# Order of the first loads, one decay on ScalarE and a two-bank last output in a retention + gated MLP kernel

## The chip, the cores and the metric

The kernel runs on 1 core of a Trainium2 chip. The metric is the device time of one execution in microseconds, and a kernel's time is the median over several executions. The engines named below are PE (TensorE, matrix multiply; PEld is its weight load), DVE (VectorE), ACT (ScalarE), POOL (GpSimd) and SP (SyncE, which here only issues DMAs). DMAs issued by SP and ACT go through the hardware queues, those issued by POOL through the software queue.

## The reference

A retention recurrence over q, k, v of shape (batch 4, heads 8, sequence 768, head dimension 64), followed by a two-layer network on the 3072 tokens:

```python
gamma = 1.0 - 2.0 ** (-5.0 - np.arange(H))
scale = 1.0 / np.sqrt(D)
for t in range(S):
    state = gamma[None, :, None, None] * state + np.einsum('bhd,bhe->bhde', k[:, :, t], v[:, :, t])
    y[:, :, t] = scale * np.einsum('bhd,bhde->bhe', q[:, :, t], state)
x = y.transpose(0, 2, 1, 3).reshape(B * S, H * D)     # 3072 x 512
h = x @ w_in                                          # 512 x 2048
g = h * np.cos(h)
out = g @ w_out                                       # 2048 x 512
```

Inputs and output are float32; the matrix work is done in bf16.

## The kernel before

The recurrence is computed in chunks of C = 128 positions. A *pair* p is one chunk of two batches (b = 0 and 1); there are 12 pairs, and six per couple of batches. Two pairs make a *group* g of 512 tokens for the network; there are 6 groups. The order of all instructions on each engine is the order in which the code issues them: nothing reorders them, and each engine works its own list in order.

For one pair:

- `load` (L108, its DMA at L113) brings q, k or v of one batch, 128 positions x 8 heads x 64, 256 KB.
- `conv_q` (L163) multiplies q by gamma^t times the scale, `conv_v` (L168) multiplies v by gamma^-t, `conv_k` (L174) casts k to bf16. gq and gk are small tables of [128 positions, chunk, head]. In the start, q is done by DVE, k by ACT and v by POOL.
- `stage_t` (L189) transposes q and k on PE, four transposes for q and four for k of each batch; `copy_bits` (L179) brings them from PSUM to SBUF on DVE. `stage_a` (L215) multiplies keys by queries, `stage_m` (L223) puts the causal mask on the product on DVE, four operations per pair.
- `half_y` (L236, L241) computes one batch's output of the pair on PE from the masked product, the decayed v and, from the second chunk on, the state; ACT copies it as `xt` (L245). `stage_s` (L257) adds to the state, which is copied at L262.

For the network: `unit_f` (L284) is one 128-row block of the hidden layer for a whole group, `pair_f` (L296) the same for one pair's 256 tokens, two blocks at a time; `act` takes the cosine on ACT (L275) and the product on DVE (L279). `unit_o` (L310) is a quarter of one 128-token block of the output; after the fourth quarter ACT copies it (L322) and SP sends it (L323). The very last block is copied in two halves of 256 columns, one by DVE (L317) and sent by SP (L318), one by ACT (L319) and sent by ACT (L320); both halves lie in one PSUM bank.

The weights come from POOL's queue, cast to bf16 on the way: `load_w_in(r)` (L118) brings a quarter of w_in, `load_w_out(r)` (L123) a quarter of w_out. `warm(n)` (L332) is n matmuls of 512 columns on zeros into a spare bank, which fill waits of PE.

The start, in the order of the code: SP loads pair 0's q0, k0, q1 and pair 1's q0; POOL loads pair 0's k1, computes two small position tables (iota), then loads pair 0's v0, v1 and pair 1's q1, k0, k1, v0, v1, then the first slice of w_in, then multiplies pair 0's v0 and v1, loads two more slices of w_in, multiplies pair 1's v0 and v1, and goes on with the last slice, w_out and pair 2. On PE: eight fillers, pair 0's transposes with fillers between, its products, its outputs, pair 1's transposes and products, then pair_f(0, 0) and half_y(1, b) in turns, stage_s(1), pair_f(1, 0), and from there unit_f and unit_o without a stop. After 48 us the transposes of later pairs are DMA transposes on SP.

PSUM banks are handed out by a first-in first-out list (`Banks`). A DMA of POOL's queue uses one of eight semaphores in turn, so that its ninth DMA waits for the first to have landed.

Of the kernel before, what the change touches and what calls it, by code (L numbers as in the profile page):

```python
# [12 lines left out]
AF = mybir.ActivationFunctionType  # L13
# [17 lines left out]
def kernel(  # L31
# [9 lines left out]
    nc = tc.nc  # L41
    B, H, S, D = q.shape
    C = 128
    NC = S // C
# [4 lines left out]
    KOUT = DF // 128  # L49
    NP = B // 2 * NC  # L50
    NG = NP // 2
# [3 lines left out]
    scale = 1.0 / math.sqrt(D)  # L55
# [8 lines left out]
    def sb(shape, dt, name):  # L64
        return const.tile(shape, dt, name=name)

    banks = Banks([psum.tile([128, 512], FP32, name=f"bank{i}") for i in range(7)])
# [10 lines left out]
    w_out_sb = sb([128, KOUT, DM], BF16, "w_out_sb")  # L78
# [4 lines left out]
    vf = [[sb([128, H, D], FP32, f"vf{i}_{b}") for b in range(2)] for i in range(PRE)]  # L83
    ob = [sb([128, DM], FP32, f"ob{i}") for i in range(4)]
    NB = 3
    qk = [sb([128, 2, 2, H, D], BF16, f"qk{i}") for i in range(NB)]
    vs = [sb([128, 2, H, D], BF16, f"vs{i}") for i in range(NB)]
# [5 lines left out]
    gt = [sb([128, KOUT, 4 * C], BF16, f"gt{i}") for i in range(2)]  # L93
# [5 lines left out]
    gk = sb([128, NC, H], FP32, "gk")  # L99
# [8 lines left out]
    def load(eng, p, names):  # L108
        bp, c = divmod(p, NC)
        for n in names:  # L110
            t, src = SRC[n[0]]
            b = int(n[1])
            eng.dma_start(  # L113
                out=t[SLOT[p]][b],
                in_=src[2 * bp + b, :, ds(c * C, C)].rearrange("h t d -> t h d"))

    def load_w_in(r):
        nc.gpsimd.dma_start(  # L118
            out=w_in_sb[r],
            in_=moe_w_in[:, ts(r, 512)].rearrange("(i p) f -> p i f", p=128))  # L120
# [6 lines left out]
    def w_in_t(i, f):  # L127
        return w_in_sb[f // 4][:, i].rearrange("p (m j) -> p j m", j=4)[:, f % 4, :]


    load(nc.sync, 0, ("q0", "k0", "q1"))
    load(nc.sync, 1, ("q0",))
    load(nc.gpsimd, 0, ("k1",))
    nc.gpsimd.iota(pos, pattern=[[C, NC]], base=1, channel_multiplier=1,
                   allow_small_or_imprecise_dtypes=True)
    nc.gpsimd.iota(rel, pattern=[[1, 128]], base=0, channel_multiplier=-1,
                   allow_small_or_imprecise_dtypes=True)
    load(nc.gpsimd, 0, ("v0", "v1"))
    load(nc.gpsimd, 1, ("q1", "k0", "k1"))
    nc.vector.memset(zero, 0.0)  # L140
    nc.vector.memset(lnsc, math.log(scale))
    nc.vector.memset(halfpi, math.pi / 2.0)
# [15 lines left out]
    def bc(g, c):  # L158
        return g[:, c, :].unsqueeze(2).to_broadcast([128, H, D])
# [6 lines left out]
    def conv_v(p, eng, bs=(0, 1), g=None):  # L166
        for b in bs:
            eng.tensor_tensor(out=vs[p % NB][:, b], in0=vf[SLOT[p]][b],  # L168
                              in1=bc(gk if g is None else g, p % NC), op=ALU.mult)
# [8 lines left out]
    def copy_bits(out, bank):  # L178
        nc.vector.tensor_scalar(out=out.bitcast(mybir.dt.uint32),  # L179
                                in0=bank.bitcast(mybir.dt.uint32),  # L180
                                scalar1=0, scalar2=None, op0=ALU.bitwise_or)

    def stage_t(p, b, fill=0):
        n = p % NB
        bank = banks.take()
        tr = bank.bitcast(BF16).rearrange("p (w a t) -> p w a t", w=2, a=HP)
        for w in range(2):
            for a in range(HP):
                nc.tensor.transpose(tr[:, w, a, :], qk[n][:, b, w, 2 * a : 2 * a + 2, :], ident)  # L189
            if w == 0:  # L190
                warm(fill)
        copy_bits(qkt[n][:, b], tr)
        banks.give(bank)
# [8 lines left out]
    def qt(n, b, a):  # L202
        return qkt[n][:, b, 0, a, :]
# [16 lines left out]
    def stage_m(p, item, parts=(0, 1)):  # L220
        b, bk, ap = item
        for j in parts:
            nc.vector.tensor_tensor(  # L223
                out=am[p % 2][b][j], in0=ap[j],
                in1=mask.unsqueeze(1).to_broadcast([128, HP, 128]), op=ALU.mult)
            banks.give(bk[j])

    def half_y(p, b):
        c = p % NC
        n = p % NB  # L230
        bank = banks.take()
        yp = bank.rearrange("p (a t) -> p a t", a=HP)
        for a in range(HP):
            if c > 0:
                for j in range(2):
                    nc.tensor.matmul(  # L236
                        yp[ts(j, 64), a, :], lhsT=stb[p % 2][:, b, a, ts(j, 64)],
                        rhs=qt(n, b, a), start=True, stop=False,
                        skip_group_check=True)
            for j in range(2):  # L240
                nc.tensor.matmul(  # L241
                    yp[ts(j, 64), a, :], lhsT=vs[n][:, b, 2 * a + j, :],
                    rhs=am[p % 2][b][j][:, a, :], start=(c == 0), stop=True,
                    skip_group_check=True)
        nc.scalar.copy(out=xt[(p // 2) % 2][:, :, ts(2 * (p % 2) + b, C)], in_=yp)  # L245
        banks.give(bank)
# [25 lines left out]
    def act(bank, out):  # L272
        cb = cosb[f_no[0] % 3]
        f_no[0] += 1
        nc.scalar.activation(out=cb, in_=bank, func=AF.Sin, bias=halfpi)  # L275
        if len(out.shape) == 3:
            cb = cb.rearrange("p (f t) -> p f t", f=2)
            bank = bank.rearrange("p (f t) -> p f t", f=2)
        nc.vector.tensor_tensor(out=out, in0=bank, in1=cb, op=ALU.mult)  # L279
# [9 lines left out]
    def pair_f(p, r, parts=(0, 1)):  # L289

        g, hf = divmod(p, 2)
        for f in [4 * r + 2 * i for i in parts]:
            bank = banks.take()
            for e in range(2):
                for i in range(KIN):
                    nc.tensor.matmul(bank[:, ts(e, 256)], lhsT=w_in_t(i, f + e),  # L296
                                     rhs=xt[g % 2][:, i, ts(hf, 256)],
                                     start=(i == 0 and e == 0), stop=(i == KIN - 1),
                                     skip_group_check=True)
            act(bank, gt[g % 2][:, f : f + 2, ts(hf, 256)])  # L300
            banks.give(bank)
# [3 lines left out]
    def unit_o(g, j, part):  # L305
        if part == 0:
            o_bank[j] = banks.take()
        bank = o_bank[j]
        for f in range(4 * part, 4 * part + 4):
            nc.tensor.matmul(bank, lhsT=gt[g % 2][:, f, ts(j, 128)], rhs=w_out_sb[:, f, :],  # L310
                             start=(f == 0), stop=(f == KOUT - 1))
        if part == 3:
            o = ob[j % 4]
            bp, c = divmod(2 * g + j // 2, NC)
            dst = out[ds((2 * bp + j % 2) * S + c * C, C), :]
            if g == NG - 1 and j == 3:
                nc.vector.tensor_copy(out=o[:, ts(0, 256)], in_=bank[:, ts(0, 256)])  # L317
                nc.sync.dma_start(out=dst[:, ts(0, 256)], in_=o[:, ts(0, 256)])  # L318
                nc.scalar.copy(out=o[:, ts(1, 256)], in_=bank[:, ts(1, 256)])  # L319
                nc.scalar.dma_start(out=dst[:, ts(1, 256)], in_=o[:, ts(1, 256)])  # L320
            else:
                nc.scalar.copy(out=o, in_=bank)  # L322
                nc.sync.dma_start(out=dst, in_=o)  # L323
            banks.give(bank)

# [2 lines left out]
    def warm(n):  # L330
        for _ in range(n):
            nc.tensor.matmul(spare, lhsT=zero[:, :128], rhs=zero, start=True, stop=True,  # L332
                             skip_group_check=True)

    def attend(p):
        for it in [stage_a(p, b) for b in range(2)]:
            stage_m(p, it)

    load(nc.gpsimd, 1, ("v0", "v1"))
    load_w_in(0)  # L340
    conv_v(0, nc.gpsimd)
    load_w_in(1)
    load_w_in(2)

    warm(8)
    conv_q(0, nc.vector)
    conv_k(0, True)
    stage_t(0, 0, 3)
    warm(2)
    stage_t(0, 1)  # L350
    a00 = stage_a(0, 0)
    stage_m(0, a00)
# [25 lines left out]
    warm(1)  # L378
    banks.give(spare)
    pair_f(0, 0, (0,))  # L380
    half_y(1, 0)
    pair_f(0, 0, (1,))
    half_y(1, 1)
    stage_s(1, nc.scalar.copy)
    pair_f(1, 0)
# [78 lines left out]
    for g in range(2, NG + 1):  # L464
        for s in range(16):
            hf, r = divmod(s, 8)
            p = 2 * (g + 1) + hf
            if g == 2 and s % 2 == 0:
                unit_o(1, *divmod(8 + s // 2, 4))
            if g < NG:  # L470
                unit_f(g, s)
            if g > 2:
                unit_o(g - 1, *divmod(s, 4))
            if p < NP:
                if r == 0:
                    ahead(p + 1)
                elif r == 1:
                    todo = [stage_a(p, b) for b in range(2)]
                    stage_m(p, todo[0])
                    if p + 1 < NP:  # L480
                        stage_t_dma(p + 1)
                elif r == 2:
                    stage_m(p, todo[1])
                elif r == 5:
                    later(p)
# [30 lines left out]
```

## Time and profile before

| what | value |
|---|---|
| median of 6 runs | 211.1 us (210.83 to 211.58) |
| the profiled execution | 211.16 us, of which the span is 209.4 us |
| mean granted TensorE clock | 0.996 |
| PE busy (share of the span) | 200.2 us (96%) |
| DVE, ACT, POOL busy | 114.8, 111.7, 91.9 us |
| HBM read, written | 27.26 MB, 6.29 MB |

The span runs from the first to the last instruction; the rest of the time lies around it. Times in the profile's rows are microseconds from the span's start. A busy row of PE is from a matmul's start to its modelled end, so that neighbouring matmuls overlap: 512 columns have a mean of 379 ns, while 16 of them in a row take about 3.45 us.

The first 30 us are also full of DMA: the page's 40 slices (5.2 us each) show 145, 335, 253, 207, 217 and 251 GB/s for the first six.

### The profile page before, as it was taken

The numbers are of one execution on the slowest core, as the hardware profiler recorded it, in microseconds if no ns is written. First come the engines' busy times: TensorE is split into PE (matmuls) and PEld (weight loads), VectorE is DVE, ScalarE is ACT, GpSimd is POOL, SyncE is SP. The second block draws the span as 40 slices with busy tenths as digits, with TensorE's granted clock in tenths as the row PEclk, the third lists the DMA queues.
The fourth block names the chain that finished last, engine by engine and source line by source line (L and its number), as shares of the span: only waits on it lengthen the run. The fifth ranks groups of instructions, "written<-read, shape, count | busy, mean of one in ns | idle before, by whom it ended". The sixth has DMA issues, their size and how long they took to land.

```text
span 209.4 us, 4140 instructions
## 1 busy us (share of the span) xinstructions
PE 200.2 (96%) x1613; PEld 112.3 (54%) x1637; DVE 114.8 (55%) x190; ACT 111.7 (53%) x181; POOL 91.9 (44%) x105
## 2 busy tenths in 40 slices
PE   7789999999999999999999999999999999999992
PEld 3258554558897554555545455455455444444440
DVE  5695785363967737859575475485382334443000
ACT  6266774237998336766745745735535553553110
POOL 7998238399997944999973400000000000000000
PEclk9999999999999999999999999999999999999998
DMA  6999999999999999999997171171101101110121
GB/s 145 335 253 207 217 251 288 333 247 333 237 254 214 223 308 279 210 274 237 285 185 178 58 95 52 51 102 50 50 3 50 50 13 41 50 50 29 73 89 64
DMA packets 49124, 33.83 MB, mean 162 GB/s; under 512 B 40080, under 2 KB 42384, under 8 KB 49104
## 3 DMA queue, kind: packets, MB, share of 16 engines
q1 hardware_dynamic: 42192, 15.86, 34.7%
q0 software_dynamic: 6768, 17.57, 31.0%
q8 instruction: 13, 0.21, 0.4%
q10 hardware_dynamic: 144, 0.13, 0.2%
q14 instruction: 7, 0.06, 0.1%
HBM read 27.26 MB, written 6.29 MB: 160 GB/s over the span
## 4 chain that ended last, share of the span: by engine, by line
PE 90%; POOL 3%; DMA 3%; issue 1%; ACT 0%; DVE 0%; POOLq 0%; DVEq 0%
PE bank L310 40%; PE bank L284 31%; PE bank L296 9%; DMA w_in<-in_moe_w_in_dram 3%; PE bank L236 3%; PE bank L215 3%; PE bank L241 2%; POOL vf L113 2%; POOL kf L113 1%; PE st_ps L257 1%; PE bank L189 1%; POOL qf L113 0%; ACT xt L245 0%; DVE ob L317 0%; ACT ob L319 0%
## 5 line engine op out<-in xcount | busy, mean ns | idle before, releaser
L279 DVE TENSOR_TENSOR gt<-bank,cosb 128x512 bf16<-128x512 f32 x96 | 65.7, 690 | 64.3 <-ACT cosb L275 63.9
L275 ACT ACTIVATE cosb<-bank,halfpi 128x512 bf16<-128x512 f32 x96 | 65.6, 687 | 52.4 <-PE bank L284 41.3
L310 PE MATMUL bank<-w_out_sb,gt 128*128 128x512 bf16 x372 | 91.8, 379 | 1.1 <-issue 0.5
L284 PE MATMUL bank<-xt,w_in 128*128 128x512 bf16 x294 | 73.7, 380 | 0.4
L310 PEld LDWEIGHTS <-gt 128*128 128x128 bf16 x384 | 36.7, 98 | 42.8
L284 PEld LDWEIGHTS <-w_in 128*128 128x128 bf16 x304 | 33.8, 114 | 30.8 <-issue 0.2
L223 DVE TENSOR_TENSOR am<-bank,mask 128x512 bf16<-128x512 f32 x48 | 30.3, 682 | 0.4 <-PE bank L215 0.2
L163 POOL TENSOR_TENSOR qk<-qf,gq 128x512 bf16<-128x512 f32 x18 | 19.1, 1081 | 15.1 <-DMA qf<-in_q_dram 15.0
L322 ACT COPY ob<-bank 128x512 f32<-128x512 f32 x23 | 13.4, 587 | 21.7 <-PE bank L310 21.4
L168 POOL TENSOR_TENSOR vs<-vf,gk 128x512 bf16<-128x512 f32 x22 | 22.5, 1046 | 0.1
L113 POOL DMA_DIRECT2D vf<-in_v_dram x23 | 20.3, 887 | 4.9 <-DMA w_out_sb<-in_moe_w_out_dram 4.9
L113 POOL DMA_DIRECT2D kf<-in_k_dram x23 | 20.8, 908 | 2.0 <-DMA w_out_sb<-in_moe_w_out_dram 1.2
L174 ACT CAST qk<-kf 128x512 bf16<-128x512 f32 x24 | 13.9, 614 | 11.8 <-DMA kf<-in_k_dram 11.6
L296 PE MATMUL bank<-xt,w_in 128*128 128x256 bf16 x160 | 18.7, 273 | 0.7 <-ACT xt L245 0.4
L296 PEld LDWEIGHTS <-w_in 128*128 128x128 bf16 x160 | 17.1, 114 | 1.5 <-DMA w_in<-in_moe_w_in_dram 0.6
L245 ACT CAST xt<-bank 128x512 bf16<-128x512 f32 x24 | 13.0, 587 | 3.0 <-DVE gt L279 3.0
L241 PE MATMUL bank<-am,vs 128*64 128x128 bf16 x192 | 11.7, 220 | 0.7 <-POOL vs L168 0.7
L241 PEld LDWEIGHTS <-vs 128*64 128x64 bf16 x192 | 9.9, 110 | 2.1 <-POOL vs L168 2.1
L236 PEld LDWEIGHTS <-stb 128*64 128x64 bf16 x160 | 8.6, 109 | 4.0 <-issue 3.5
L236 PE MATMUL bank<-qkt,stb 128*64 128x128 bf16 x160 | 10.5, 222 | 0.0
L262 DVE CAST stb<-st_ps 64x512 bf16<-64x512 f32 x12 | 8.2, 687 | 3.5 <-PE st_ps L257 3.3
L332 PE MATMUL bank<-gt 128*128 128x512 bf16 x19 | 7.8, 525 | 1.4 <-DVE gt L140 1.2
(36 smaller groups left out, 65.0 us busy)
## 6 DMA issues: line engine op xcount, KB each, us to landing
kf<-in_k_dram POOLq DMA_DIRECT2D x23, 256.0 KB, 5.6
vf<-in_v_dram POOLq DMA_DIRECT2D x23, 256.0 KB, 6.8
out_dram<-ob SPq DMA_DIRECT2D x23, 256.0 KB, 2.0
qf<-in_q_dram SPq DMA_DIRECT2D x19, 256.0 KB, 6.7
w_in<-in_moe_w_in_dram POOLq DMA_DIRECT2D x4, 512.0 KB, 8.1
w_out_sb<-in_moe_w_out_dram POOLq DMA_DIRECT2D x4, 512.0 KB, 12.5
qf<-in_q_dram POOLq DMA_DIRECT2D x5, 256.0 KB, 7.5
kf<-in_k_dram SPq DMA_DIRECT2D x1, 256.0 KB, 4.8
```

Source lines behind the costliest of these rows:

```text
L113: eng.dma_start(out=t[SLOT[p]][b], in_=src[2 * bp + b, :, ds(c * C, C)].rearrange("h t d -> t h d"))
L163: eng.tensor_tensor(out=qk[p % NB][:, b, 0], in0=qf[SLOT[p]][b], in1=bc(gq, p % NC), op=ALU.mult)
L168: eng.tensor_tensor(out=vs[p % NB][:, b], in0=vf[SLOT[p]][b], in1=bc(gk if g is None else g, p % NC), op=ALU.mult)
L174: nc.scalar.copy(out=qk[p % NB][:, b, 1], in_=kf[SLOT[p]][b])
L223: nc.vector.tensor_tensor(out=am[p % 2][b][j], in0=ap[j], in1=mask.unsqueeze(1).to_broadcast([128, HP, 128]), op=ALU.mult)
L236: nc.tensor.matmul(yp[ts(j, 64), a, :], lhsT=stb[p % 2][:, b, a, ts(j, 64)], rhs=qt(n, b, a), start=True, stop=False, skip_group_check=True)
L241: nc.tensor.matmul(yp[ts(j, 64), a, :], lhsT=vs[n][:, b, 2 * a + j, :], rhs=am[p % 2][b][j][:, a, :], start=(c == 0), stop=True, skip_grou ...
L275: nc.scalar.activation(out=cb, in_=bank, func=AF.Sin, bias=halfpi)
L279: nc.vector.tensor_tensor(out=out, in0=bank, in1=cb, op=ALU.mult)
L284: nc.tensor.matmul(bank, lhsT=w_in_t(i, f), rhs=xt[g % 2][:, i, :], start=(i == 0), stop=(i == KIN - 1))
L296: nc.tensor.matmul(bank[:, ts(e, 256)], lhsT=w_in_t(i, f + e), rhs=xt[g % 2][:, i, ts(hf, 256)], start=(i == 0 and e == 0), stop=(i == KIN ...
L310: nc.tensor.matmul(bank, lhsT=gt[g % 2][:, f, ts(j, 128)], rhs=w_out_sb[:, f, :], start=(f == 0), stop=(f == KOUT - 1))
```

## The change

Four things:

- The hardware queue brings only pair 0's q0 and k0 in the start. POOL's queue brings, in this order, pair 0's q1, (the two iotas,) pair 0's k1, v0, v1, pair 1's q0, k0, q1, k1, the first slice of w_in, then, behind the multiply of pair 0's v1, pair 1's v0 and v1, and the next two slices of w_in.
- Pair 0's v0 is multiplied by ACT, in eight operations of one head each, behind the casts of pair 0's k; v1 stays on POOL.
- Two fillers of PE go (one in pair 0's first stage_t, one behind it), and pair_f(0, 0) does both its halves ahead of half_y(1, 0).
- The last 128-token block of the output is no longer four quarters of unit_o into one bank: `last_o` takes 320 columns into one bank and then 192 columns into another. ACT copies and SP sends the first, DVE copies and ACT sends the second.

```diff
-    load(nc.sync, 0, ("q0", "k0", "q1"))
-    load(nc.sync, 1, ("q0",))
-    load(nc.gpsimd, 0, ("k1",))
+    load(nc.sync, 0, ("q0", "k0"))
+    load(nc.gpsimd, 0, ("q1",))
     nc.gpsimd.iota(pos, pattern=[[C, NC]], base=1, channel_multiplier=1,
                    allow_small_or_imprecise_dtypes=True)
     nc.gpsimd.iota(rel, pattern=[[1, 128]], base=0, channel_multiplier=-1,
                    allow_small_or_imprecise_dtypes=True)
-    load(nc.gpsimd, 0, ("v0", "v1"))
-    load(nc.gpsimd, 1, ("q1", "k0", "k1"))
+    load(nc.gpsimd, 0, ("k1", "v0", "v1"))
+    load(nc.gpsimd, 1, ("q0", "k0", "q1", "k1"))
+    load_w_in(0)
...
-            if g == NG - 1 and j == 3:
-                nc.vector.tensor_copy(out=o[:, ts(0, 256)], in_=bank[:, ts(0, 256)])
-                nc.sync.dma_start(out=dst[:, ts(0, 256)], in_=o[:, ts(0, 256)])
-                nc.scalar.copy(out=o[:, ts(1, 256)], in_=bank[:, ts(1, 256)])
-                nc.scalar.dma_start(out=dst[:, ts(1, 256)], in_=o[:, ts(1, 256)])
+            nc.scalar.copy(out=o, in_=bank)
+            nc.sync.dma_start(out=dst, in_=o)
+            banks.give(bank)
+
+    def last_o(g, j):
+        bp, c = divmod(2 * g + j // 2, NC)
+        dst = out[ds((2 * bp + j % 2) * S + c * C, C), :]
+        for i, (a, n) in enumerate(((0, 320), (320, 192))):
+            bank = banks.take()
+            for f in range(KOUT):
+                nc.tensor.matmul(bank[:, :n], lhsT=gt[g % 2][:, f, ts(j, 128)],
+                                 rhs=w_out_sb[:, f, ds(a, n)],
+                                 start=(f == 0), stop=(f == KOUT - 1))
+            o = ob[i]
+            if i:
+                nc.vector.tensor_copy(out=o[:, :n], in_=bank[:, :n])
+                nc.scalar.dma_start(out=dst[:, ds(a, n)], in_=o[:, :n])
             else:
-                nc.scalar.copy(out=o, in_=bank)
-                nc.sync.dma_start(out=dst, in_=o)
-            banks.give(bank)
+                nc.scalar.copy(out=o[:, :n], in_=bank[:, :n])
+                nc.sync.dma_start(out=dst[:, ds(a, n)], in_=o[:, :n])
...
+    conv_v(0, nc.gpsimd, (1,))
     load(nc.gpsimd, 1, ("v0", "v1"))
-    load_w_in(0)
-    conv_v(0, nc.gpsimd)
     load_w_in(1)
     load_w_in(2)
 
     warm(8)
     conv_q(0, nc.vector)
     conv_k(0, True)
-    stage_t(0, 0, 3)
-    warm(2)
+    for h in range(H):
+        nc.scalar.activation(out=vs[0][:, 0, h, :], in_=vf[0][0][:, h, :], func=AF.Copy,
+                             scale=gk[:, 0, h : h + 1])
+    stage_t(0, 0, 2)
+    warm(1)
     stage_t(0, 1)
...
     pair_f(0, 0, (0,))
+    pair_f(0, 0, (1,))
     half_y(1, 0)
-    pair_f(0, 0, (1,))
     half_y(1, 1)
...
             if g > 2:
-                unit_o(g - 1, *divmod(s, 4))
+                if g < NG or s < 12:
+                    unit_o(g - 1, *divmod(s, 4))
+                elif s == 12:
+                    last_o(g - 1, 3)
```

## The prediction

> **What bounds the kernel now.** I read the chain of waits first, since it tells in order of time what set the end. Columns: start in us, length in us, what.
>
> ```profile
> 5.38 1.75 POOL kf L113 x2
> ...
> 8.88 6.81 DMA w_in<-in_moe_w_in_dram
> 15.73 1.06 PE bank L296 x8
> ...
> 18.98 0.59 ACT xt L245
> 19.61 1.91 PE bank L296 x16
> 21.57 10.31 PE bank L284 x47
> ...
> 204.18 1.47 PE bank L310 x6
> 205.73 0.43 DVE ob L317
> 206.19 0.37 ACT ob L319
> ```
>
> From 19.61 us to 205.65 the chain is matrix work almost alone, back to back; the change adds and removes nothing in there. What can move is the start, up to 19.61, and the tail after the last matmul. The start hangs by this view on GpSimd's issues and the first w_in slice. I then read the timeline engine by engine to see what else would hold the start (columns: start, length, engine, line, operation; in brackets the idle time before it and who ended it).
>
> ```profile
> 15.05 0.39 PE L332 MATMUL bank<-gt 128*128 128x512 bf16 x1
> 15.73 1.06 PE L296 MATMUL bank<-xt,w_in 128*128 128x256 bf16 x8 [0.29 <-DMA w_in<-in_moe_w_in_dram]
> ...
> 19.61 1.91 PE L296 MATMUL bank<-xt,w_in 128*128 128x256 bf16 x16 [0.43 <-ACT xt L245]
> ```
>
> The chain overstates w_in: without it PE, done with its filler at 15.44, would have gone on 0.29 us sooner. What brought PE there so late is VectorE:
>
> ```profile
> 6.97 0.69 DVE L163 TENSOR_TENSOR qk<-qf,gq 128x512 bf16<-128x512 f32 x1 [2.47 <-DMA qf<-in_q_dram]
> 7.58 1.49 DVE L179 TENSOR_SCALAR qkt<-bank 128x512 uint32<-128x512 uint32 x2
> 8.99 2.47 DVE L223 TENSOR_TENSOR am<-bank,mask 128x512 bf16<-128x512 f32 x4
> 11.38 1.49 DVE L163 TENSOR_TENSOR qk<-qf,gq 128x512 bf16<-128x512 f32 x2
> ...
> 14.50 2.48 DVE L223 TENSOR_TENSOR am<-bank,mask 128x512 bf16<-128x512 f32 x4 [0.22 <-PE bank L215]
> ```
>
> It waits 2.47 us for pair 0's second q and then works nearly without a gap to 16.98. So two things must both come earlier: that q with pair 0's k, and the w_in slice.
>
> **Part 1, the loads.** GpSimd issues eight loads ahead of w_in's first slice before and after: two come from the hardware queue (pair 0's q1, pair 1's q0), two leave (pair 1's v0, v1). Its issue stays at 8.88. What changes is what moves ahead of it: in the DMA view by narrow windows, the hardware queue moved 1.05 MB (four loads) until 8 us, now two loads; so w_in's first slice is the 11th transfer and no longer the 13th. Issue to landing, same view: k1 4.8 us (lands 6.1), v0 5.0 (7.7), v1 5.7 (9.3), pair 1's k1 5.4 (11.6), v0 5.3 (12.4), v1 5.2 (13.2), w_in 6.8 (15.7). From 9 to 13 us, with GpSimd's queue alone, a load takes 0.75 to 0.8 us and a w_in slice 2.5. The shortest landing of any kf load behind 60 us is 3.9 us from the issue's start; I take it as floor, and the landing of the same place in the old order as ceiling. The issues are 0.88 us each (0.94 for the one after the iotas).
>
> - pair 0: k0 (hardware queue) by 6.05 as before, q1 5.3 to 6.1 (was 6.97), k1 6.6 to 7.7 (was 6.1), v0 7.5 to 9.3, v1 8.4 to 10.2.
> - pair 1: q0 9.3, k0 10.2, q1 11.0, k1 11.9 (was 11.6); then w_in 14.4 (11.9 + 2.5; was 15.7), v0 15.2, v1 15.9 (was 13.2). The next slice waits behind the same bytes as before: 19.0 to 19.2, needed at about 20.5.
>
> The Trainium skill, page "DMA: Bandwidth & Descriptors", section "Issuing engines are not separate DMA queues", says that all issuers share the same 16 DMA engines and that spreading DMAs over issuers saves issue time only. The split by queue agrees on sharing, with 283 to 349 GB/s in total between 6 and 8 us whichever queue moved more. By that rule alone the move costs two more software issues and wins nothing; the gain here is the order in the queue, which the rule does not touch.
>
> **Part 2, pair 0's v by ScalarE.** One POOL multiply goes (L168, 1.05 us), eight ScalarE operations of 128x64 come. No row shows one; the nearest are the 128x48 exponentials, 0.34 and 0.23 us, 0.24 apart. Eight by 0.24 to 0.34 is 1.9 to 2.7; I take 2.1, as consecutive ones overlap in those rows. They run from 7.5 to 9.6, where ScalarE was idle (3.76 us before 10.95), so cost nothing; without that cover the casts of pair 1's k behind them would be late by what sticks out. With v0 at 9.3 they end at 11.4, and half_y(0, 0) comes 0.6 later than its 10.77. The second v stays on POOL: 9.65 to 10.7, as the old first multiply.
>
> **Part 3, VectorE's chain.** q1's scaling ends by 6.75 and k0's transposes by 7.1, so the first copy_bits runs at 7.1 instead of 7.6. k1's cast 6.65 to 7.25, transposes by 7.7, second copy 7.75 to 8.4, masks 8.4 to 10.9 (were 8.99 to 11.46), pair 1's scalings to 12.2. Pair 1's k1 cast ends at 12.5, its transposes at 13.0, copies to 13.7; the second masks start at about 14.0, not 14.50 (with k1 at its ceiling of 7.7: 14.5). PE is through its filler 0.8 to 0.9 after that: 14.8. The first w_in slice is there at 14.4, so pair_f starts at 14.8 instead of 15.73.
>
> **Part 4, both halves of pair_f ahead of half_y(1, 0).** Same instructions, other order. From the second half's start to its cosine on ScalarE it was 17.29 to 18.39, 1.10 us; ScalarE gives 0.59 to a cosine before its next instruction and 1.07 to two xt copies, and PE followed 0.05 later. A half is 0.88 of matmuls. So from pair_f to pair_f(1, 0): 0.88 + 1.10 + 0.59 + 1.07 + 0.05 = 3.69, against 3.88 now: 0.2 won.
> Behind it POOL now holds pair 1's v: its multiplies wait for v0 and v1 (15.2 and 15.9) and end at 16.2 and 17.25, where half_y(1, 1) needs the second at 14.8 + 2.4 = 17.2. A tie. Queued behind these multiplies stand w_in's last slice and w_out, issued from 17.3 instead of 15.27; the queue is then still moving slices 2 and 3 (the old third one landed at about 21.5), so nothing starves.
>
> Start: 14.8 + 3.7 = 18.5, or 18.6 by the v's, against 19.61: 1.0 at best. With the landings at their ceilings pair_f stays at 15.73 and Part 4's 0.2 is left. I take 0.85, nearer the floors because two transfers fewer compete.
>
> **Part 5, the tail.** The last output's 16 matmuls of 512 columns become 16 of 320 and 16 of 192. Steps in the rows: 216 ns at 512 (0.86 for 4), 109 at 256 (1.75 for 16), 56 at 128: 137 and 82 by the line through them, 3.50 us instead of 3.45, 0.05 lost (0.3 if each of the 16 added weight loads cost 16 ns more). Before, two copies ran one after the other, because one bank held both:
>
> ```profile
> 205.73 0.42 DVE L317 COPY ob<-bank 128x256 f32<-128x256 f32 x1 [13.32 <-PE bank L310]
> 206.19 0.33 SPq L318 DMA_DIRECT2D out_dram<-ob  x1
> 206.19 0.37 ACT L319 COPY ob<-bank 128x256 f32<-128x256 f32 x1 [3.38 <-DVE ob L317]
> 206.59 0.37 ACTq L320 DMA_DIRECT2D out_dram<-ob  x1
> ```
>
> Now the first bank is copied and sent while PE does the second (1.3 us of cover), and only VectorE's copy of 192 columns is left: 0.42 less 64 by 1.03 ns (the step from 256 columns to 512, 0.42 to 0.69) = 0.36. The last transfer is issued at 205.78 + 0.36 + 0.04 = 206.18 instead of 206.59: 0.41 won, 0.2 to 0.5 by the bounds. The landing (1.7 us) and the 1.1 us behind it stay.
>
> **Sum.** 0.85 + 0.41 = 1.26 off the profiled execution's 211.16 (span 209.4 and 1.76 around it): span 208.1, time 209.9. The median of the runs is 211.1, so the two agree.
>
> **Part 6, two fillers fewer.** The 512-column fillers go at 0.43 us a step from 1.19 to about 5.9 and at 0.21 from 6.96, the four transposes take 0.63 at 4.58 and 0.40 at 6.72, while the granted clock reads 1.00 in every half microsecond. The doubling came between, after 5.3 us of unbroken work. Now PE stops at about 6.0 and waits for k0's cast until 6.7. I cost this at nothing, because everything PE does from 7 to 14 hides behind VectorE; if PE stayed at half rate it would cost what the third rival says.
> The Trainium skill, "TensorE: Matmul & The Clock Gate", Part 1, gives the rule against this edit: the array runs at half rate until a free-running activity window of about 3.4 us was busy. The steps agree with a halved rate. By the rule 4.8 us of work still hold a whole window for most phases, so the sum stays; a missed window would add half-rate work up to the next.
>
> **Rivals.**
> 1. Only the tail gains. Pair 1's v lands at 17.1 instead of 15.9 (or w_in no earlier than 15.7 and VectorE no earlier either), half_y(1, 1) starts at 18.25 and pair_f(1, 0) at 19.6. For it: the v's sit behind 1 MB of source data and a tie has no slack. Against: the bytes ahead of v1 equal those that were through at 15.7 before. Time 211.16 - 0.41 = 210.75, or 210.5 with Part 4.
> 2. The start's gain is eaten later, by PE running into slices or k and q of pair 2. Against: w_in 2 to 4 and w_out landed 2.2 to 4.5 us before their use, pair 2's q was scaled at 35.2 for transposes at 39.5. Time again 210.75.
> 3. Slower: PE has no full rate when pair_f begins. Then 16 matmuls of 109 ns double (+1.7) and half_y(1) too (+0.9); less 0.6 of slack under ScalarE and the tail's 0.4: 211.16 + 1.6 = 212.8. It decides from the point where PE's steps are still 0.43 at 14.8 us; a delay that ends by 11 costs at most 0.5. For it: a 0.7 us hole in the first spell of work. Against: the eight fillers before it are untouched.
>
> **How the numbers follow.** Forecast (209.2 to 210.6) 0.70; rivals 1 and 2 together (210.4 to 211.2) 0.16; rival 3 and a still later v 0.14. A change under 0.2%, 0.42 us, can't be told from none. Faster, below 210.7: 0.70 and 0.06 of rival 1. Slower, above 211.5: 0.13. Same 0.11. The range 209.2 to 211.2 leaves out 0.14 above and a little below.
>
> **What would show it.** pair_f's first matmul near 14.8 and pair_f(1, 0) near 18.6; masks at 8.4 and 14.0; no ScalarE wait for v beyond 8; the last issue 0.5 after the last matmul. I am wrong if pair_f(1, 0) starts behind 19.3, if half_y(1, 1) waits for POOL's multiply by more than 0.3, if fillers still step at 0.43 behind 7 us, or if PE shows waits for DMA after 20.

## The result and the profile after

| | before | after |
|---|---|---|
| median of all runs | 211.87 us (62 runs, 210.83 to 216.15) | 213.53 us (27 runs, 211.97 to 218.54) |
| ratio after / before, 95% interval | | 1.0075 [1.0058, 1.0093] |
| profiled execution, its span | 211.16, 209.4 us | 212.69, 210.9 us |
| start of pair_f(0, 0) | 15.73 us | 17.34 us |
| start of pair_f(1, 0) | 19.61 us | 21.55 us |
| start of unit_f (the stretch without a stop) | 21.57 us | 23.51 us |
| end of the last matmul | 205.65 us | 207.63 us |
| issue of the last transfer | 206.59 us | 208.10 us |

The kernel became slower by 0.6 to 0.9%, against a forecast of 0.6% faster. All ratios here compare executions in the chip's usual state, while the profiles of extra_hw, order_only and decay_only below are of slower ones (216.07, 215.76 and 216.64 us), so that of these three only the start is read. The table gives the account: 1.94 us lost up to unit_f, 184.1 us of matrix work in the middle in both, 0.04 lost in the last block, and 0.94 - 0.47 = 0.47 won between the last matmul and the last issue. 1.94 + 0.04 - 0.47 = 1.51, which is the 1.5 between the spans.

The chain of waits of the kernel after, first 24 us (start, length, what):

```profile
8.88 0.77 POOL w_in L118
9.65 0.99 POOL vs L168
10.64 7.41 DMA vf<-in_v_dram
...
18.19 2.05 POOL vs L168 x2
...
20.91 0.59 ACT xt L245
...
21.55 1.91 PE bank L296 x16
```

One piece of 7.41 us, pair 1's v0, stands where the chain of before had the w_in slice. POOL then multiplies it, and half_y(1, 1) and pair_f(1, 0) come behind. The chain shows only what ended last. The timeline of PE shows that the w_in slice was late too (start, length, engine, line, operation; in brackets the idle time before and who ended it):

```profile
15.16 0.39 PE L343 MATMUL bank<-gt 128*128 128x512 bf16 x1
17.34 1.94 PE L296 MATMUL bank<-xt,w_in 128*128 128x256 bf16 x16 [1.79 <-DMA w_in<-in_moe_w_in_dram]
...
20.29 0.25 PE L241 MATMUL bank<-am,vs 128*64 128x128 bf16 x2 [0.37 <-POOL vs L168]
...
21.55 1.91 PE L296 MATMUL bank<-xt,w_in 128*128 128x256 bf16 x16 [0.43 <-ACT xt L245]
```

PE had ended its filler at 15.55 and stood still for 1.79 us until the first slice had landed. That wait, 0.29 in before, is most of the loss. The transfers themselves, from the DMA view by windows of 0.1 us or less, one issue each (KB, us from issue to landing): pair 1's k1, the slice behind it, pair 1's v0:

```profile
kf<-in_k_dram POOLq DMA_DIRECT2D x1, 256.0 KB, 4.6
...
w_in<-in_moe_w_in_dram POOLq DMA_DIRECT2D x1, 512.0 KB, 8.4
...
vf<-in_v_dram POOLq DMA_DIRECT2D x1, 256.0 KB, 7.4
```

Issued at 8.00, 8.88 and 10.64, they landed at 12.6, 17.3 and 18.05. So the slice needed 4.7 us beyond the load ahead of it, where before it needed 2.5. The queue's line for 13 to 15 us (packets, MB, time of the packets as a share of 16 engines), first of before, run again beside the others,

```profile
q0 software_dynamic: 415, 0.41, 123.9%
```

then of after:

```profile
q0 software_dynamic: 257, 0.28, 108.2%
```

The queue was occupied for nearly as large a part, but moved a third less: single packets took longer. In the packet records of before, run again, no packet of this queue between 8 and 16 us took over 195 ns, and the slice's 1 KB packets took 98 ns; in after 33 took over 400 ns, the longest 1859. Nothing else was moving between 13 and 15 us: q0 is the only queue listed there.

The tail did what was forecast:

```profile
206.38 0.43 ACT L334 COPY ob<-bank 128x320 f32<-128x320 f32 x1 [1.63 <-PE bank L326]
206.83 0.33 SPq L335 DMA_DIRECT2D out_dram<-ob  x1
207.71 0.36 DVE L331 COPY ob<-bank 128x192 f32<-128x192 f32 x1 [13.36 <-PE bank L326]
208.10 0.37 ACTq L332 DMA_DIRECT2D out_dram<-ob  x1
```

The first bank's copy begins 1.3 us before the second's, and the second takes 0.36 + 0.03 us from there to its issue.

### The profile page after: what moved, and what is told of

Read it like the earlier page. It is cut to its first block, busy times and chain, and to the rows that moved or that the text cites. A ratio compares the mean times of both kernels' runs of the same rounds, so it can differ in the third digit from the quotient of the medians.

```text
span 210.9 us, 4178 instructions
## 1 busy us (share of the span) xinstructions
PE 200.6 (95%) x1628; PEld 114.0 (54%) x1651; DVE 114.7 (54%) x190; ACT 114.1 (54%) x189; POOL 92.4 (44%) x106
## 4 chain that ended last, share of the span: by engine, by line
PE 88%; POOL 5%; DMA 4%; issue 1%; ACT 0%; DVE 0%; POOLq 0%; DVEq 0%
PE bank L310 38%; PE bank L284 31%; PE bank L296 8%; DMA vf<-in_v_dram 4%; PE bank L215 3%; PE bank L236 3%; PE bank L241 2%; PE bank L326 2%; POOL vs L168 1%; POOL qf L113 1%; POOL kf L113 1%; PE st_ps L257 1%; PE bank L189 1%; POOL vf L113 1%; POOL w_in L118 0%
## 5 line engine op out<-in xcount | busy, mean ns | idle before, releaser
L310 PE MATMUL bank<-w_out_sb,gt 128*128 128x512 bf16 x357 | 88.4, 379 | 1.1 <-issue 0.5
L310 PEld LDWEIGHTS <-gt 128*128 128x128 bf16 x368 | 35.1, 98 | 40.8
L168 POOL TENSOR_TENSOR vs<-vf,gk 128x512 bf16<-128x512 f32 x21 | 21.5, 1045 | 4.2 <-DMA vf<-in_v_dram 4.2
L241 PE MATMUL bank<-am,vs 128*64 128x128 bf16 x192 | 12.3, 220 | 0.4 <-POOL vs L168 0.4
L215 PE MATMUL bank<-qkt 64*128 64x128 bf16 x192 | 8.0, 218 | 0.7 <-DVE qkt L179 0.5
```

Of the source, the lines that this page charges most:

```text
L215: nc.tensor.matmul(ap[j][:, a, :], lhsT=kt(n, b, a)[po : po + 64, :], rhs=qt(n, b, a)[po : po + 64, :], tile_position=(po, 0))
L241: nc.tensor.matmul(yp[ts(j, 64), a, :], lhsT=vs[n][:, b, 2 * a + j, :], rhs=am[p % 2][b][j][:, a, :], start=(c == 0), stop=True, skip_grou ...
```

## The experiments

The question was why the slice took 4.7 us. The expectations call the theories by letters where they need them. **L**: the slice and pair 1's v land late, and this is the loss. **Q**: the software queue had too little work waiting ahead of the slice, because POOL's issues now feed it with nearly every byte it moves. **B**: bandwidth, more bytes or packets competing ahead of it. **W**: the new place of the slice, ahead of pair 1's v. **D**: a disturbance from outside, which would hit before too. All ratios are to before on the same chip, with 95% intervals. Each diff stands against after, unless it says before.

### Before and after once more

No edit in either.

> The kernel before, unchanged, for a second profile and as a control. Theory L (the changed kernel loses at the start because the first w_in slice and pair 1's v land late) and theory D (the slow landings of its profile are a disturbance of the memory from outside, which the kernel before suffers as well): ratio 1.000. Theory D in addition: single DMA packets of 1 us and more around 11 to 15 us, and the first w_in slice later than 15.7 us. Theory L: the slice lands near 15.7 us again.

> The changed kernel, unchanged, for a second profile. Theory L: ratio 1.007 again, the first w_in slice lands 2 to 3 us later than the 14.4 us forecast, pair_f starts near 17. Theory D: in a profile without long packets the slice lands near 14.4 us, pair_f starts near 15.5 and the span is 1 us under that of the kernel before.

Measured: before 0.9981 [0.995, 1.0012], after 1.0098 [1.0063, 1.0132]. On one chip, before had its slice at 15.65 and after at 17.5; after's long packets came again (22 over 400 ns from 8 to 16 us, none in before). D falls.

### The loads as before, all else as after (old_loads)

```diff
-    load(nc.sync, 0, ("q0", "k0"))
-    load(nc.gpsimd, 0, ("q1",))
+    load(nc.sync, 0, ("q0", "k0", "q1"))
+    load(nc.sync, 1, ("q0",))
+    load(nc.gpsimd, 0, ("k1",))
...
-    load(nc.gpsimd, 0, ("k1", "v0", "v1"))
-    load(nc.gpsimd, 1, ("q0", "k0", "q1", "k1"))
-    load_w_in(0)
+    load(nc.gpsimd, 0, ("v0", "v1"))
+    load(nc.gpsimd, 1, ("q1", "k0", "k1"))
...
-    conv_v(0, nc.gpsimd, (1,))
     load(nc.gpsimd, 1, ("v0", "v1"))
+    load_w_in(0)
+    conv_v(0, nc.gpsimd, (1,))
```

> The changed kernel with the loads as before (four in the hardware queue, pair 1's v ahead of the first w_in slice), and with ScalarE's half of v, the two fillers fewer, pair_f's halves together and the tail as changed. Theory L: the whole loss is in the loads, so 210.5 or less against 211.1, ratio 0.995 to 0.998, pair_f(1, 0) near 19.4. Rival P (the loss is in the order of pair_f and half_y or in ScalarE's eight operations): ratio 1.005 or more, pair_f(1, 0) behind 20.5.

Measured: 0.994 [0.9912, 0.9968], median 210.94, span 208.8. PE's timeline:

```profile
15.89 1.94 PE L296 MATMUL bank<-xt,w_in 128*128 128x256 bf16 x16 [0.66 <-DMA w_in<-in_moe_w_in_dram]
...
19.57 1.91 PE L296 MATMUL bank<-xt,w_in 128*128 128x256 bf16 x16 [0.47 <-ACT xt L245]
```

The slice landed at 15.85, 2.4 us behind its forerunner, and the whole loss was gone. The other three parts are worth 0.3 to 0.9% together; the loads took that and more away.

### The new loads alone on before (loads_only)

Against before: the loads of after, with all else as in before, so POOL multiplies both v of pair 0.

```diff
-    load(nc.sync, 0, ("q0", "k0", "q1"))
-    load(nc.sync, 1, ("q0",))
-    load(nc.gpsimd, 0, ("k1",))
+    load(nc.sync, 0, ("q0", "k0"))
+    load(nc.gpsimd, 0, ("q1",))
...
-    load(nc.gpsimd, 0, ("v0", "v1"))
-    load(nc.gpsimd, 1, ("q1", "k0", "k1"))
+    load(nc.gpsimd, 0, ("k1", "v0", "v1"))
+    load(nc.gpsimd, 1, ("q0", "k0", "q1", "k1"))
+    load_w_in(0)
...
-    load(nc.gpsimd, 1, ("v0", "v1"))
-    load_w_in(0)
     conv_v(0, nc.gpsimd)
+    load(nc.gpsimd, 1, ("v0", "v1"))
```

> The kernel before with the changed loads alone (two in the hardware queue, the first w_in slice ahead of pair 1's v; both v's of pair 0 stay on GpSimd, between that slice and pair 1's v). Theory L: the loss of the changed kernel without the tail's gain, ratio 1.009 to 1.015, the first w_in slice at 17 us or later. If the ratio is under 1.003, the loads need the rest of the change to lose.

Measured: 1.0146 [1.0055, 1.0238], from four executions. The slice landed at 17.0, 4.8 us behind its forerunner, and pair_f(1, 0) started at 23.33. The loads alone cause the loss. In this profile PE fell to half rate as well:

```profile
17.09 1.06 PE L296 MATMUL bank<-xt,w_in 128*128 128x256 bf16 x8 [1.65 <-DMA w_in<-in_moe_w_in_dram]
...
19.92 1.89 PE L296 MATMUL bank<-xt,w_in 128*128 128x256 bf16 x8
```

The same eight matmuls take 1.06 us, and after the waits 1.89. This adds to the loss here, but does not make it: the profile is of the longest of the four executions (216.65 us), and the two with a mean granted clock of 0.997 and 1.00 took 214.42 and 214.02, still 1.1 to 1.3% above before. After, with the same loads, loses less because the other three parts win 0.3 to 0.9% back.

### Two q back in the hardware queue, the slice still ahead of v (q_in_hw)

```diff
-    load(nc.sync, 0, ("q0", "k0"))
-    load(nc.gpsimd, 0, ("q1",))
+    load(nc.sync, 0, ("q0", "k0", "q1"))
+    load(nc.sync, 1, ("q0",))
+    load(nc.gpsimd, 0, ("k1",))
...
-    load(nc.gpsimd, 0, ("k1", "v0", "v1"))
-    load(nc.gpsimd, 1, ("q0", "k0", "q1", "k1"))
+    load(nc.gpsimd, 0, ("v0", "v1"))
+    load(nc.gpsimd, 1, ("q1", "k0", "k1"))
     load_w_in(0)
```

> The changed kernel with pair 0's q1 and pair 1's q0 back in the hardware queue; the first w_in slice stays ahead of pair 1's v. Theory Q (the software queue, with eight loads of its own and few in the other queue, never has transfers waiting, and its packets then stall; with a backlog they run evenly): packets even again, the slice lands near 14.2 us, pair 1's v near 16, ratio 0.992 to 0.996. Rival W (the slice ahead of the v's is what hurts, by the order alone): slice and v's late as in the changed kernel, PE waits for POOL's multiply, ratio 1.003 or more.

Measured: 0.9966 [0.9925, 1.0008]. The slice, issued at 7.12, landed at 14.4, 2.5 us behind its forerunner, with pair 1's v at 15.1 and 16.2. The order slice before v does no harm: W falls. What differs from after is the queue of two loads. pair_f began at 16.18, held by VectorE's chain and not by the slice: the granted clock was 0.57 from 10 to 12 us and 0.58 from 12 to 14. It fell in half of the executions: the five with a mean granted clock of 1.00 have a median of 209.97 us, the five with 0.992 or less 212.36.

### v ahead of the slice, two loads in the hardware queue (v_first)

```diff
     load(nc.gpsimd, 1, ("q0", "k0", "q1", "k1"))
+    load(nc.gpsimd, 1, ("v0", "v1"))
     load_w_in(0)
...
     conv_v(0, nc.gpsimd, (1,))
-    load(nc.gpsimd, 1, ("v0", "v1"))
     load_w_in(1)
```

> The changed kernel with two loads in the hardware queue, but pair 1's v ahead of the first w_in slice again. Theory Q: the queue still has no backlog, packets stall, the slice (issued at 10.6 us) lands at 18 us or later, ratio 1.005 or more. Rival W: the order as before, no loss, the slice near 16 us, ratio 0.994 to 0.998.

Measured: 1.0174 [1.0081, 1.0266], from four executions. The counterpart: old order of slice and v, new queues, and the slice again needed 4.9 us (14.3 to 19.2).

```profile
19.23 3.28 PE L297 MATMUL bank<-xt,w_in 128*128 128x256 bf16 x16 [3.20 <-DMA w_in<-in_moe_w_in_dram]
...
24.25 1.91 PE L297 MATMUL bank<-xt,w_in 128*128 128x256 bf16 x16 [0.47 <-ACT xt L246]
```

Sixteen matmuls of pair_f took 3.28 us where they take 1.91 otherwise, after a wait of 3.2.

### q_in_hw with v issued ahead of POOL's multiply (q_hw_v_early)

The edit of q_in_hw, and in addition:

```diff
-    conv_v(0, nc.gpsimd, (1,))
     load(nc.gpsimd, 1, ("v0", "v1"))
+    conv_v(0, nc.gpsimd, (1,))
```

> As the one with the two q's back in the hardware queue, and pair 1's v issued ahead of GpSimd's multiply of pair 0's v1, so that the software queue never runs short. Theory Q: pair 1's v about 0.5 us earlier than there, the same ratio or 0.001 lower. Rival W: as late as there.

Measured: 0.9936 [0.9912, 0.996], median 210.27, span 208.5.

```profile
15.12 1.91 PE L297 MATMUL bank<-xt,w_in 128*128 128x256 bf16 x16
...
19.10 1.91 PE L297 MATMUL bank<-xt,w_in 128*128 128x256 bf16 x16 [0.43 <-ACT xt L246]
```

The slice landed at 14.8 and pair_f started at 15.12 with no wait. Pair 1's v landed at 15.6 and 16.4, later than in q_in_hw by 0.5 and 0.2 and not 0.5 earlier as expected; the slice ahead of them was 0.5 later too. This version beats before and after; it can't be told from old_loads (0.994), so the slice's new place is worth little by itself. From pair_f to pair_f(1, 0) it took 3.98, not 3.68: half_y(1, 1) waited 0.19 us for POOL's multiply of pair 1's v.

### More traffic ahead of the slice (extra_hw)

After, with pair 2's q0 and q1 brought early by the hardware queue: POOL's list up to the slice is untouched, and 512 KB more move ahead of it.

```diff
     load(nc.sync, 0, ("q0", "k0"))
+    load(nc.sync, 2, ("q0", "q1"))
     load(nc.gpsimd, 0, ("q1",))
...
-    load(nc.gpsimd, 2, ("k0", "q0", "k1", "q1"))
+    load(nc.gpsimd, 2, ("k0", "k1"))
```

> The changed kernel with pair 2's q0 and q1 brought by the hardware queue in the start, behind pair 0's k0; they were the 19th and 21st load of GpSimd's queue. So there is 512 KB more to move ahead of the first w_in slice. Theory Q (the software queue needs transfers waiting ahead of the one that moves): the added transfers slow the software queue early, its loads then wait for their turn and run evenly; the slice lands at 15.7 us instead of 17.3 although more goes ahead of it, ratio 0.996 to 1.002. Rival B (the start is short of bandwidth, or the two q's are slower in the software queue whatever goes beside): the slice lands later than 17.3, ratio 1.009 or more.

Here Q and B say opposite things. Measured: 1.002 [0.9987, 1.0054]. The queue's line for 13 to 15 us:

```profile
q0 software_dynamic: 393, 0.46, 123.9%
```

It moves 0.46 MB, against 0.28 in after, and no packet of it took over 347 ns from 8 to 16 us. The slice, issued at 8.87 (8.88 in after; KB, us from issue to landing):

```profile
w_in<-in_moe_w_in_dram POOLq DMA_DIRECT2D x1, 512.0 KB, 6.9
```

It landed at 15.8, 1.5 us **earlier** than in after, with 512 KB more ahead of it; it needed 2.5 us. B falls. The kernel is still no better than before: pair_f starts at 16.62 without any wait for DMA, held by VectorE's chain. Pair 0's k1 landed at 7.9 (in after 6.7) and pair 1's at 13.3 (12.6), and the granted clock was 0.60 from 10 to 12 us and 0.54 from 12 to 14. All 12 executions have a mean granted clock of 0.992 or less, so the ratio holds a loss that is not the slice's; between Q and B the landing decides.

### One load back (one_back)

```diff
     load(nc.sync, 0, ("q0", "k0"))
+    load(nc.sync, 1, ("q0",))
     load(nc.gpsimd, 0, ("q1",))
...
-    load(nc.gpsimd, 1, ("q0", "k0", "q1", "k1"))
+    load(nc.gpsimd, 1, ("k0", "q1", "k1"))
     load_w_in(0)
```

> The changed kernel with one load, pair 1's q0, back in the hardware queue (three there). Theory Q: seven software loads ahead of the w_in slice, issued at 8.0 us, backlog between the two kernels; fewer long packets, the slice at 14.5 to 16 us, ratio 0.995 to 1.003. Rival: no step of the ratio in between, 1.007 as with both moved.

Measured: 0.9962 [0.9928, 0.9996]; the slice needed 3.7 us, between the others. In the profile taken, pair_f started at 17.59 and not when the slice was there (15.5): pair 0's k1 landed at 8.0 (in after 6.7), and the granted clock was 0.50 from 10 to 14 us and 0.55 from 14 to 16, so that 16 transposes on PE took 1.91 us (1.06 in extra_hw). So this run's slice belongs in the table below, and its ratio says little on the queue.

### Each remaining part alone on before

tail_only: the new last output. order_only: pair_f(0, 0)'s second half ahead of half_y(1, 0), nothing else. decay_only: pair 0's first v on ScalarE and two fillers fewer.

> The kernel before with the last output in two banks alone. Both theories: 0.41 us less, ratio 0.998; the last DMA is issued 0.46 us behind the last matmul instead of 0.94. If the ratio is 1.000 or above, the tail is not worth what the profile shows.

> The kernel before with both halves of pair_f ahead of half_y(1, 0) alone. By the forecast's Part 4: from pair_f to pair_f(1, 0) 3.69 us instead of 3.88, 0.2 us less, ratio 0.999; the rival (half_y late makes ScalarE's xt copies late): 4.2 us or more, ratio 1.002.

> The kernel before with ScalarE's eight operations in place of GpSimd's multiply of pair 0's v0, and the two fillers fewer. By the forecast: eight operations in 2.1 us, hidden; PE's start is set by the w_in slice at 15.7, so ratio 1.000 and pair_f(0, 0) at 15.7. The rival: the casts of pair 1's k or a half-rate array make it later, ratio 1.003 or more.

Measured: tail_only 0.9985 [0.9957, 1.0012]; the expected 0.998 lies inside, and so does 1. The profile decides better: there 0.48 us lie between last matmul and last issue, 0.94 in before. order_only 0.9971 [0.9943, 0.9998]; in its profile pair_f to pair_f(1, 0) is 16.19 to 19.87, 3.68 us. But pair_f itself began 0.46 later than in before, so this profile shows the step and not the gain. decay_only 0.9989 [0.995, 1.0029]: half_y(0, 0) ran at 9.99 instead of 10.77 and nothing behind it moved, with pair_f at 15.87. Hidden.

### What the runs say together

For each run: which loads the hardware queue had moved early, how long after the end of the slice's issue its forerunner landed (the lead the slice had), and how long it then took to land. The last column counts the software queue's packets of over 400 ns that began between 8 and 16 us.

| kernel | loads by hardware queue | lead, us | slice behind its forerunner, us | long packets |
|---|---|---|---|---|
| q_hw_v_early | 4 | 4.4 | 2.5 | 1 |
| q_in_hw | 4 | 4.0 | 2.5 | 16 |
| old_loads | 4 | 3.8 | 2.4 | 0 |
| extra_hw | 4 | 3.6 | 2.5 | 0 |
| before_again | 4 | 3.5 | 2.5 | 0 |
| one_back | 3 | 3.0 | 3.7 | 15 |
| after | 2 | 2.9 | 4.7 | 33 |
| v_first | 2 | 2.9 | 4.9 | 30 |
| after_again | 2 | 2.7 | 5.2 | 22 |
| loads_only | 2 | 2.6 | 4.8 | 35 |

For the first slice a lead of 3.5 us or more gives 2.4 to 2.5 us whatever the order and the kernel; at 3.0 and below it is 3.7 to 5.2. (The first profile of before, tail_only, order_only and decay_only, all with four loads, have leads of 3.5 to 4.0 and 2.5 us.) Of q_in_hw's 16 long packets 13 have the 4 KB of a load and 3 the 1 KB of a slice. The 13 began between 12.8 and 14.9 us, the time of pair 1's v, so loads are held up in the same way; of after's 33 it is 22 and 11.

The later slices don't all follow this. The second slice of q_in_hw does: with four loads on the hardware queue, but a lead of only 2.8 us, it needed 4.7. But second slices needed 4.0 at a lead of 3.8 (one_back) and 3.5 at 6.0 (v_first), and fourth slices at leads of 2.8 needed 3.2 (after) and 2.5 (after_again). So the lead sorts the first slices of these kernels, and is not shown to be a rule for any transfer.

Why the lead went follows from two rates. POOL issues a load every 0.88 us (256 KB, 0.298 MB/us). The software queue moved about 0.34 MB/us in before once it had the DMA engines alone (a load every 0.75 to 0.8 us). With four loads on the hardware queue, the software queue's early loads wait behind those bytes and about 3.5 us of work stand in line. With two the software queue starts moving at once, and its eight loads then land 0.93 to 1.02 us apart on average (after, after_again, loads_only): near POOL's 0.88, not at the queue's 0.75 to 0.8, and no such line builds up.

## Why the prediction was wrong

**The step that failed** is in Part 1, "then w_in 14.4 (11.9 + 2.5; was 15.7), v0 15.2, v1 15.9". The 2.5 us of a slice, like the 0.75 to 0.8 of a load, were read between 9 and 13 us of before, from a queue with 3.5 us of work in line, and laid on a queue whose line the change itself shortened. Measured: 17.3, 18.05 and 18.8. Of the 2.9 us between 14.4 and 17.3, 0.7 come from the forerunner and 2.2 from the slice. The reason given for landings near the floor, "because two transfers fewer compete", had the sign wrong: with the hardware queue's bytes there, the slice took 2.5 us, without them 4.7.

**The 0.7** is a size in the same step: pair 1's k1 landed at 12.6 instead of 11.9. I had used the floor of 3.9 us from issue to landing, seen behind 60 us; here the four loads of pair 1 took 4.3 to 4.6. With it VectorE's second masks began at 14.61 and not at 14.0 (Part 3), and PE was ready at 15.55 and not at 14.8 (0.94 behind the masks' start, as in before's rows, where the prediction took 0.8). VectorE's timeline:

```profile
8.41 2.47 DVE L223 TENSOR_TENSOR am<-bank,mask 128x512 bf16<-128x512 f32 x4
...
14.61 2.48 DVE L223 TENSOR_TENSOR am<-bank,mask 128x512 bf16<-128x512 f32 x4 [0.22 <-PE bank L215]
```

The first masks were right to 0.01 us, the second had lost the lead again. So even with a slice of 2.5 us, landing at 15.1, pair_f could have begun no earlier than 15.55, 0.18 before the old kernel, plus 0.2 from Part 4: by these rows at most 0.4 of the forecast 0.85 were there. The sign of the result comes from the late slice and the late v behind it: without them these rows leave a gain at the start and 0.43 at the tail.

**Part 4** was right in its 3.69 (3.68 in order_only and old_loads). In after it took 4.21 (17.34 to 21.55), because the tie forecast for pair 1's v became a wait: POOL began its multiplies at 18.19, not 15.2, and PE stood 0.37 for them. The bound set for that wait, 0.3, was passed.

**Part 2** held: ScalarE's eight operations took 2.02 us from 7.98, forecast 2.1 from 7.5, and decay_only shows them hidden. **Part 5** held: 0.47 less 0.04, forecast 0.41. **Part 6** held in after's profile: pair_f ran at full rate, 1.94 us for its 16 matmuls. Its "for most phases" does not follow, though: by the 3.4 us that it goes by, 4.8 us of work hold a whole window in (4.8 - 3.4) / 3.4 of the phases, an estimate of two in five. In q_in_hw, extra_hw and one_back, which lack the same two fillers, PE stood still for 1.1 to 1.2 us between 6.9 and 8.7 us, and the clock fell behind it; in old_loads, which lacks them too, PE stood 1.44 us from 6.3 us on and the clock stayed at 1.00. No run leaves out the fillers alone, so what they are worth stays open.

**The rivals.** Rival 1 named the right place, pair 1's v too late and w_in no earlier, but stopped at no loss: it set w_in's latest landing at the old 15.7, as Part 1 had taken "the landing of the same place in the old order as ceiling". That bound was false. Rival 3 had the right sign by the wrong cause in after's profile; its mechanism, PE at half rate, did appear in loads_only and v_first, behind PE's wait for the slice, and in q_in_hw, extra_hw and one_back from about 9 or 10 us on, ahead of the slice.

**Weighing the rule.** I had noted that by the Trainium skill, page "DMA: Bandwidth & Descriptors", section "Issuing engines are not separate DMA queues", the move to POOL costs issues and wins nothing, and set it aside for the order of the queue. Against the gain I forecast, it was the better guide. But its reason, that the choice of the issuer only saves issue time, does not cover what happened: in extra_hw POOL's issues up to the slice are unchanged and the transfer still went from 4.7 to 2.5 us.

**Open.** Shown is that with two loads on the hardware queue the first slice stalls packet by packet, and that a longer line ahead of it cures that. What the packets wait for is not in the trace; that the queue catches up with POOL's writing of the descriptors is a guess, and no run tried it, nor whether POOL's or VectorE's work at that time has a part in it.

The medians of old_loads and after differ by 2.6 us where their profiled spans differ by 2.1. The clocks on record account for the rest. Of the 23 executions of after that the ratio uses, 15 have a mean granted clock of 0.997 or more and a median of 212.9 us, and 8 have 0.992 or less and 214.2; of old_loads' 12 one has 0.992, and the other eleven have a median of 210.9. At the full clock the difference is 2.0. Of the 83 executions of before that the ratios of the experiments use, none is below 0.996. Where in the start or behind it the clock fell in those 8 is not on record; old_loads lacks the same fillers, which makes PE's wait for the slice the likelier cause, but no more.

## What to carry to other kernels

A transfer's duration read from a trace belongs to the backlog it had there: before moving loads between queues, work out how much will stand in line at the moment the important transfer's turn comes, and price it by a row with the same lead. If one engine issues nearly all bytes at a rate below what the queue can move (here 0.298 against 0.34 MB/us), no line builds up and each transfer follows its issue at about POOL's pace; here two loads left on the other queue were worth more than they cost. A bound like "no later than in the old order" has to be shown, since changing the order changes the rate too.

## What the runs showed of the hardware

- More traffic made a transfer land earlier: 512 KB added on the hardware queue brought the slice from 17.3 to 15.8 us.
- The software queue's packets are not of a fixed length: 98 ns for the slice's 1 KB and up to 195 ns for a load's 4 KB in a queue with a line; in one without, up to 1818 ns for the first (v_first) and 1859 ns for the second (after), with no other queue listed in the window of after.
- PE's rate fell after one wait of 3.2 us in v_first. It fell in loads_only too, where from 10 to 19 us no wait was longer than 1.65 us; that one was followed by 1.2 us of work and a wait of 0.70. The table of stretches of loads_only ends with granted clock, DMA share and GB/s; the clock is 0.73 and 0.50:

```profile
18.00:20.00 2.00, 1.30 (x19) 0.91 (x18) 0.69 (x1) 0.69 (x1) 1.75 (x2) 0.73 1.22 207
20.00:22.00 2.00, 2.00 (x14) 1.20 (x16) 0.00 (x0) 0.73 (x2) 2.00 (x4) 0.50 1.22 197
```

The Trainium skill, "TensorE: Matmul & The Clock Gate", section "HAM oscillation — how this bites in real kernels", puts the rule as no idle gap of PE above about 3.4 us. v_first lies near that figure; loads_only, by its rows, fell well under it. After waited 1.79 us and, run again, 2.27, and kept its clock both times, so a wait of this length sometimes costs and sometimes doesn't.
